# ScalarE's program as a loop over four packs, V loaded by one transfer per pack, and two kinds of transfer moved to SyncE's queue, in a cached two-block attention kernel

## The chip, the cores and the metric

One core of one Trainium2 chip. The time is device microseconds of one execution. Three runs of the kernel before took 739.08, 739.24 and 739.37 us, median 739.24. The profiled execution took 739.09 us, of which the profile's span covers 737.3.

## The reference

Two blocks A and B of the same form, with inputs of their own, side by side in the last dimension of the output. B = 16 batches, Sq = 64 queries, D = 640, H = 32 heads, Sk = 512 keys, Dh = 128, all bf16.

```
q = (x @ wq).reshape(B, Sq, H, Dh).transpose(0, 2, 1, 3)
scores = einsum("bhqd,bhkd->bhqk", q, k_cache) * Dh**-0.5
p = softmax(scores)
o = einsum("bhqk,bhkd->bhqd", p, v_cache)
out = o.transpose(0, 2, 1, 3).reshape(B, Sq, H * Dh) @ wo
```

The K and V caches of both blocks are 268 MB of the 292 MB that the kernel reads.

## The kernel before

**Packs, groups, phases.** A pack is two batches times four heads; there are 128, and each brings 1 MB of K and 1 MB of V. Four packs (NJ = 4) make a group: the same two batches, sixteen heads, one accumulated output. Eight groups (all 16 batches) make a phase of 32 packs: half of the heads of one block. Phases 0 and 1 are block A, 2 and 3 block B. Each phase has weights of its own: wq (five transfers LDWQ, put in order by POOL's WP) and wo (four transfers LDWO of 640 KB, one for each pack position).

**Operations of pack n.** LDK and LDV bring K and V (before: two transfers of 512 KB each, with K in four for the first eight packs). On TensorE: QP (query projection, L626), S (scores, L650), TR (transposes of the probabilities, L709), PV (L732), OP (output projection, L752), and once per group XT (transposes of x, L605). On VectorE: KT (two blockwise transposes of K, L640), RC (two reciprocals of row sums, L682), TE (two copies of the transposed probabilities out of PSUM, L719), once per group OS (the output's sum, L762 and L765). On ScalarE: QE (L632), four EX (exponentials with row sums, L669), two OE (L740), ZO (zeroes a PSUM region, L744), and XE (x out of PSUM, L611) in the groups of the first phase of each block. On POOL: four NM (probabilities times reciprocal, L698), once per group XC (L615). ST stores a group's output in phases 1 and 3.

**The order.** `build_plan` gives each operation a place in time, in units of one pack, from the table `AT` (S of pack n at n, TR at n + 1.293 and so on). Sorted by it, the operations make one fixed program for each engine; the loads make SP's program, sorted by keys given at `loads.append`. Each engine runs its program in order. TensorE's round is S(m), TR(m-1), OP(m-2), [XT,] QP(m+1), PV(m-1). VectorE's is KT(m+1), TE(m-1,0), RC, TE(m-1,1), RC. SP's interleaves V(n), K(n+3) and the rarer loads.

**Waits.** From what each operation reads and writes the planner derives dependencies, turns them into semaphore waits, drops those that others imply, and lets one wait stand in for another where the latter's semaphore is kept for TensorE (`stand_in`). Some waits are put on an earlier operation of another engine: the wait for wo stood on OE(n,1) on ScalarE, the wait for x and for WP on EX.

**Loops.** TensorE's program is a hardware loop of 32 turns over four packs (`Fori`); at each turn it lowers its semaphores by what one turn adds, so that every turn waits for the same values. The programs of the other engines are written out in full for all 128 packs.

**Rings.** K has six buffers (NK), V four (NV). A V buffer is free again when PV of the pack four before it is done, so SP's LDV(n) waits for PV(n-4). EX writes its probabilities into `p_ring`, and NM multiplies them into the one buffer `pn_sb`, which TR reads.

**Queues.** SP issues K, V, x, wq from phase 1 on, and wo of phase 0. ScalarE issues the first loads of x and wq, wo of phases 1 to 3 (L565) and all output stores (L771). They are two hardware queues, q1 and q10 in the profile, in front of the same sixteen DMA engines.

**The end.** The last two packs (NARROW) use another layout, and the last one is normalised by VectorE instead of POOL. In the program of before, its third and fourth NM stand behind its transposes: they start at 732.00 us, TR at 728.48.

Of the kernel before, what the change touches and what calls it, by code (L numbers as in the profile page):

```python
# [17 lines left out]
PARTS = dict(d_v=2)  # L18


class Cfg:
# [5 lines left out]
    NQ = 2  # L27
    NP = 4
    NR = 2
# [5 lines left out]
    AT = dict(XT=-2.585, XE=-2.383, XC=-0.788, QP=-0.428, QE=-0.224, KT=(-0.672, -0.65), S=0,  # L35
              EX=(0.307, 0.252, 0.358, 0.4), RC=(0.45, 0.6), RCO=0.48, NM=(0.803, 0.854, 1.088, 1.187),
              NMZ=(0.615, 1.231, 1.718, 1.794), TR=1.293, TE=(1.432, 1.47), PV=1.701, OE=(1.888, 2.013), ZO=2.221,
              OP=2.387, OS=2.576, LDWO=2.6, ST=3.559, WP0=-1.75, WP1=-1.596)
# [20 lines left out]
LOADS = ("LDK", "LDV", "LDX", "LDWQ", "LDWO")  # L59


def build_plan(dims, cfg, general):
# [18 lines left out]
    def add_output(n):  # L81
        g, j = n // NJ, n % NJ
        final = n >= 0 and dims["FINAL"](g // NBP)
        for b in range(2):
            tv = n + AT["PV"]
            op = add("sp", "LDV", (n, b), tv - 0.3, [], [("v" if n >= 0 else "absent", n % cfg.NV, b)])
            loads.append((n - cfg.NV + AT["PV"] + 0.2 if n >= 0 else -99.0, 3, op))
        if n > -2:
            add("pe", "TR", n, n + AT["TR"], [("pn", i) for i in range(4)] + [("ident",)], [("B", 4), ("B", 5)])
# [17 lines left out]
    for g in range(N // NJ + 1):  # L107
        n0 = g * NJ
        txt = n0 + AT["XT"]
        add("pe", "XT", g, txt, [("xn", g % cfg.NXN), ("ident",)], [("SB", 0)])  # L110
        if g == N // NJ:
            break
        if dims["FIRST"](g // NBP):
            add("act", "XE", g, n0 + AT["XE"], [], [("SB", 0), ("xs", g % NBP)])
            if g:
                loads.append((txt - 3.7, 0, add("sp", "LDX", g, txt - 0.5, [], [("xn", g % cfg.NXN)])))
            else:
                add("act", "LDX", g, -21.0, [], [("xn", g % cfg.NXN)])
        add("pool", "XC", g, n0 + AT["XC"], [("xs", g % NBP)], [("xT", g % cfg.NX)])
    for ph in range(NPH):  # L120
# [5 lines left out]
        for j in range(NJ):  # L126
# [5 lines left out]
            if ph:  # L132
                add("act", "LDWO", w, n0 - NJ + AT["LDWO"], [], [("wo", j)])
# [7 lines left out]
    add("pool", "NM", -1, -1 + AT["NM"][3], [], [("pn", i) for i in range(4)])  # L141
    for n in range(-2, N):
# [15 lines left out]
        for i in range(4):  # L158
            h = 4 * n + i
            te = n + AT["EX"][i]  # L160
            if general:
                add("dve", "MX", h, te - 0.002, [], [("SB", i), ("negmax", h % 4)])
            add("act", "EX", h, te, [("negmax", h % 4)] if general else [],
                [("SB", i), ("p", h % cfg.NP), ("rs", h)])
            add("pool" if n < N - 1 else "dve", "NM", h, n + (AT["NM"] if n < N - 1 else AT["NMZ"])[i], [("p", h % cfg.NP), ("recip", n % cfg.NR, i // 2)], [("pn", i)])
        for a in range(2):
            add("dve", "RC", (n, a), n + (AT["RCO"] if n % NJ == 1 and not a else AT["RC"][a]), [("rs", 4 * n + i) for i in (2 * a, 2 * a + 1)],
                [("recip", n % cfg.NR, a)])
    if not general:
        add("dve", "FL1", 0, N - 1 + AT["TE"][1] + 0.002, [("rs", h) for h in range(4 * N)], [("good",)])  # L170
# [25 lines left out]
    pe = progs["pe"]  # L196
    lo = next(i for i, o in enumerate(pe) if o.kind == "QP" and o.idx == 0)
    hi = next(i for i, o in enumerate(pe) if o.kind == "QP" and o.idx == cfg.PERIOD)
    size = hi - lo
    last_qp = max(o.idx for o in pe[lo:hi] if o.kind == "QP")  # L200
    reps = 1 + (N - 1 - last_qp) // cfg.PERIOD
    step = dict(XT=cfg.PERIOD // NJ, QP=cfg.PERIOD, S=cfg.PERIOD, TR=cfg.PERIOD, PV=cfg.PERIOD, OP=cfg.PERIOD)
    for k in range(reps):
        for i in range(size):
            o, o0 = pe[lo + k * size + i], pe[lo + i]
            assert o.kind == o0.kind and o.idx == o0.idx + k * step[o.kind], (k, i, o.kind, o.idx, o0.kind, o0.idx)
    loop = dict(lo=lo, size=size, reps=reps)
    inside = {id(o) for o in pe[lo:lo + size * reps]}

    for op in ops:  # L210
        if op.kind == "OP":
            at[("OE", (op.idx, 1))].deps += [d for d in op.deps if d.kind in ("LDWO", "WZ")]
            op.deps = [d for d in op.deps if d.kind not in ("LDWO", "WZ")]
        if op.kind == "XT" and op.idx > 0:
            at[("EX", 4 * (NJ * op.idx - NJ + 1))].deps += [d for d in op.deps if d.kind == "LDX"]
            op.deps = [d for d in op.deps if d.kind != "LDX"]
        if op.kind == "QP" and op.idx > 0:
            at[("EX", 4 * op.idx - 4)].deps += [d for d in op.deps if d.kind == "WP"]
# [4 lines left out]
    def for_pe(d):  # L223
        if d.kind == "EX":
            return d.idx % 4 == 1 or d.idx % 4 == 0 and d.idx // 4 % NJ == 1
        if d.kind == "OE":
            return d.idx[1] == 0
        if d.kind == "NM":
# [5 lines left out]
    def stand_in(d, op):  # L234
        if op.eng == "pe":
# [10 lines left out]
            return d  # L246
        if not for_pe(d):
# [23 lines left out]
    def sem_key(op):  # L271
        if op.kind in ("LDX", "LDWQ") and op.eng == "act":
            return ("d_first",) + op.writes[0]
        if op.kind == "LDV":
            return ("d_v", op.writes[0][1])
# [19 lines left out]
    per = periodic_waits(progs, loop)  # L295
    verify_waits(progs, base)
    loop["per"] = per
    loop["take"] = place_takes(progs["pe"][lo:lo + size], per)
    return progs, counts, loop


def place_takes(turn, per):


    spots = [i for i, o in enumerate(turn) if o.kind == "OP"] + [len(turn) - 1]
# [96 lines left out]
def periodic_waits(progs, loop):  # L402

    pe = progs["pe"]
# [41 lines left out]
def mha_kernel(nc, blocks, out, cfg=None):  # L446
# [24 lines left out]
    NK, NV, NKT, NX, NXN, NQ, NP, NR = (cfg.NK, cfg.NV, cfg.NKT, cfg.NX, cfg.NXN, cfg.NQ, cfg.NP, cfg.NR)  # L471

    with contextlib.ExitStack() as es:
# [11 lines left out]
        xT_ring = sb("xT_ring", [128, NX, KT, 128], BF16)  # L485
        xs_sb = sb("xs_sb", [128, NBP, KT * 128], BF16)
        xn_ring = sb("xn_ring", [128, NXN, D], BF16)
        qs_ring = sb("qs_ring", [128, NQ, 4, 2, 64], BF16)
        p_ring = sb("p_ring", [128, NP, 512], BF16)
        pn_sb = sb("pn_sb", [128, 16, 128], BF16)  # L490
        pT_sb = sb("pT_sb", [128, 2, 16, 64], BF16)
        oT_sb = sb("oT_sb", [128, 4, 128], BF16)
        zeros = sb("zeros", [128, 256], BF16)
        out_sb = sb("out_sb", [128, D], BF16)
        acc = sb("acc", [128, NBP, D], F32)
        rowsum = sb("rowsum", [128, NH], F32)
        negmax = sb("negmax", [128, 4], F32)
        recip = sb("recip", [128, NR, 4], F32)
# [7 lines left out]
        for p, (_progs, counts, _loop) in enumerate(plans):  # L506
# [71 lines left out]
        def em_LDV(e, op):  # L578
# [3 lines left out]
            blk, bp, j, h = pack_info(n)  # L582
            src = blocks[blk][2][2 * bp + b, h:h + 4]
# [26 lines left out]
        def em_XE(e, op):  # L610
            ins = e.activation(xs_sb[:, op.idx % NBP, :], x_ps[:, 0:KT * 128], ACTF.Copy)  # L611
            return ins, ins

        def em_XC(e, op):
            ins = e.tensor_copy(xT_ring[:, op.idx % NX].rearrange("p k q -> p (k q)"), xs_sb[:, op.idx % NBP, :])  # L615
# [44 lines left out]

        def exp_views(h):
            src, dst = ps[:, h % 4, :], p_ring[:, h % NP, :]
            u = 2 if wide(h // 4) else 4
            return (src.rearrange("q (u t p) -> q t p u", u=u, p=16), dst.rearrange("q (t p u) -> q t p u", p=16, u=u))

        def em_EX(e, op):
            h = op.idx
            src, dst = exp_views(h)
            ins = e.activation(dst, src, ACTF.Exp, scale=1.0, accum_out=rowsum[:, h:h + 1])  # L669
            return ins, ins  # L670

        def em_EXG(e, op):
# [3 lines left out]
            ins = e.activation(dst, src, ACTF.Exp, bias=negmax[:, r:r + 1], scale=1.0, accum_out=rowsum[:, h:h + 1])  # L676
            return ins, ins

        def em_RC(e, op):
            n, a = op.idx  # L680
            lo, hi = 2 * a, 2 * a + 2
            ins = e.reciprocal(recip[:, n % NR, lo:hi], rowsum[:, 4 * n + lo:4 * n + hi])  # L682
            return ins, ins

        def em_NM(e, op):
            h = op.idx
            i = h % 4
            if h < 0:
                ins = e.memset(pn_sb[:, :, :].rearrange("p t c -> p (t c)"), 0.0)
                return ins, ins  # L690
            if wide(h // 4):
                dst = pn_sb[:, :, 32 * i:32 * i + 32]
                src = p_ring[:, h % NP, :].rearrange("q (t k) -> q t k", t=16)
            else:
                a, s = i // 2, i % 2
                dst = pn_sb[:, 8 * a:8 * a + 8, 64 * s:64 * s + 64]
                src = p_ring[:, h % NP, :].rearrange("q (t k) -> q t k", t=8)
            ins = e.tensor_scalar(dst, src, recip[:, h // 4 % NR, i:i + 1], 1.0, ALU.mult, ALU.mult)  # L698
# [5 lines left out]
        def em_TR(e, op):  # L704
            first = last = None
            for c in range(16):
                for b in range(2):
                    rows = slice(64 * b, 64 * b + 64)
                    last = e.transpose(pt_bank(b)[:, 64 * c:64 * c + 64], pn_sb[rows, c, :], ident[rows, rows],  # L709
# [33 lines left out]
        def em_ZO(e, op):  # L743
            ins = e.activation(z_ps, zeros[:, :].rearrange("p (s c) -> p s c", s=2), ACTF.Copy)  # L744
# [31 lines left out]
        def em_FL1(e, op):  # L776
            first = e.tensor_reduce(extreme[:, 0:1], rowsum[:, :], AX.X, ALU.max)
            first.then_inc(s_ch, 1)
            e.tensor_reduce(extreme[:, 1:2], rowsum[:, :], AX.X, ALU.min).then_inc(s_ch, 1)
            e.wait_ge(s_ch, 2)  # L780
            e.tensor_scalar(extreme[:, 2:3], extreme[:, 0:1], SUM_MAX, None, ALU.is_le).then_inc(s_ch, 1)
            e.tensor_scalar(extreme[:, 3:4], extreme[:, 1:2], SUM_MIN, None, ALU.is_ge).then_inc(s_ch, 1)
# [37 lines left out]
        def run_program(e, eng, p):  # L820
            progs, counts, loop = plans[p]
            prog = progs[eng]
            if eng != "pe":
                for i, op in enumerate(prog):
                    if p == 0 and i == max(0, len(prog) - 300):
                        ahead[eng] = e.mark_branch_hint_location()
                    emit(e, op, p, {})
                return
            lo, size, reps, per = loop["lo"], loop["size"], loop["reps"], loop["per"]
            for key in sorted(counts):  # L830
                if key[0].startswith("q_"):
                    e.sem_inc(sems[p][key], cfg.BASE)
            for op in prog[:lo]:
                emit(e, op, p, {})
# [105 lines left out]
```

## Time and profile before

| | before |
|---|---|
| median of three runs | 739.24 us |
| profiled execution / its span | 739.09 / 737.3 us |
| busy: PE, DVE, ACT, POOL | 678.4, 521.8, 529.6, 404.0 us |
| DMA | 295.12 MB, mean 400 GB/s |
| V loads | 256 issues of 512 KB, 14.8 us (A) and 16.5 us (B) from issue to landing |
| wo loads by ScalarE's queue | 12 of 640 KB, 17.7 us (A) and 16.9 us (B) |
| output stores | 16 of 160 KB, 6.7 us |

A matmul group's busy time is modelled, so "PE busy 92%" does not say that TensorE is the bound. The DMA row counts how busy the sixteen DMA engines were on average: at 9 in every slice they had work all the time. "q14 instruction" and "q8 instruction" are the fetches of the engines' programs, which run on the same DMA engines. Semaphores tell when a transfer has landed: it counts sixteen increments, so a reader of the tile waits for the last of them.

### The profile page before, as it was taken

The page shows a single profiled execution, that of the slowest core. Times are in us where ns is not written, and L with a number is a line of the kernel's source. Part 1 is how long each engine was busy: PE and PEld are TensorE (multiplying, and loading weights), DVE is VectorE, ACT ScalarE, POOL GpSimd, SP SyncE. Part 2 cuts the span into 40 slices and gives each one's busy share as a digit, 9 for nine tenths or more (in the row PEclk, how much of TensorE's full clock was granted, in tenths as well). Part 3 has the DMA queues.
Part 4 walks back from the last instruction along what each step waited for, and adds up shares of the span by engine and source line. Part 5 has one row for each costly group of instructions (what it writes and reads, how often), then busy time and mean ns, then how long its engine had stood idle before and what let it go on. Part 6 is the DMA issues. An engine that isn't in the chain of part 4 may idle for free.

```text
span 737.3 us, 61335 instructions
## 1 busy us (share of the span) xinstructions
PE 678.4 (92%) x28502; PEld 531.3 (72%) x28502; DVE 521.8 (71%) x818; ACT 529.6 (72%) x1559; POOL 404.0 (55%) x580
## 2 busy tenths in 40 slices
PE   3669999999998999999988989999999799999997
PEld 2457787877776777777766767777777577878785
DVE  7437877877767767767765677768686577787775
ACT  2448888888776777767766777768777577777775
POOL 3635555556964455554684644555577455555451
PEclk9999999999999999999999999999999999999999
DMA  8999999999999999999999999999999999999991
GB/s 323 393 405 414 414 414 414 413 415 414 410 402 412 417 416 415 416 417 415 414 403 407 415 414 414 414 414 413 415 416 402 409 415 416 416 416 415 417 387 38
DMA packets 75995, 295.12 MB, mean 400 GB/s; under 512 B 9520, under 2 KB 24368, under 8 KB 59568
## 3 DMA queue, kind: packets, MB, share of 16 engines
q1 hardware_dynamic: 64544, 281.41, 94.4%
q10 hardware_dynamic: 11408, 13.27, 5.1%
q14 instruction: 33, 0.27, 0.1%
q8 instruction: 10, 0.16, 0.1%
HBM read 292.03 MB, written 2.62 MB: 400 GB/s over the span
## 4 chain that ended last, share of the span: by engine, by line
PE 47%; DMA 25%; SPq 12%; DVE 5%; POOL 4%; issue 3%; ACT 2%; ACTq 0%; POOLq 0%; DVEq 0%
DMA kn_ring<-in_B_k_cache_dram 15%; PE ps L732 13%; PE ps L752 11%; PE ps L626 10%; PE ps L650 8%; DMA kn_ring<-in_A_k_cache_dram 8%; SPq L586 6%; PE ps L709 5%; SPq L575 5%; DVE kt_ring L640 3%; DMA ws_sb<-in_A_wq_dram 2%; POOL pn_sb L698 2%; POOL wqp_sb L598 2%; DVE pT_sb L719 2%; ACT p_ring L669 1%
## 5 line engine op out<-in xcount | busy, mean ns | idle before, releaser
L698 POOL TENSOR_SCALAR pn_sb<-p_ring,recip 128x512 bf16<-128x512 bf16 x508 | 341.8, 692 | 302.7 <-DVE recip L682 302.6
L640 DVE STREAM_TRANSPOSE kt_ring<-kn_ring 128x1024 f32<-128x1024 f32 x256 | 302.8, 1222 | 123.5 <-DMA kn_ring<-in_B_k_cache_dram 85.3
L669 ACT ACTIVATE p_ring<-ps 128x512 bf16<-128x512 f32 x512 | 298.0, 596 | 9.5 <-PE ps L650 5.4
L719 DVE COPY pT_sb<-ps 128x1024 bf16<-128x1024 bf16 x258 | 169.6, 669 | 52.3 <-PE ps L709 52.1
L732 PE MATMUL ps<-pT_sb,v_ring 32*128 32x64 bf16 x16512 | 163.3, 192 | 30.9 <-DVE pT_sb L719 15.5
L732 PEld LDWEIGHTS ps<-pT_sb,v_ring 32*128 32x128 bf16 x16512 | 148.5, 91 | 46.5 <-issue 26.2
L626 PE MATMUL ps<-xT_ring,wqp_sb 128*128 128x128 bf16 x2560 | 166.4, 221 | 7.2 <-POOL xT_ring L615 7.2
L740 ACT ACTIVATE oT_sb<-ps 128x256 bf16<-128x256 f32 x260 | 85.7, 381 | 120.2 <-PE ps L732 119.5
L752 PE MATMUL ps<-wo_sb,oT_sb 128*128 128x320 bf16 x1040 | 166.8, 304 | 1.7 <-ACT ps L744 1.6
L626 PEld LDWEIGHTS ps<-xT_ring,wqp_sb 128*128 128x128 bf16 x2560 | 158.0, 114 | 13.6 <-issue 7.4
L650 PE MATMUL ps<-kt_ring,qs_ring 32*64 32x512 bf16 x4096 | 139.7, 383 | 3.0 <-issue 2.9
L632 ACT ACTIVATE qs_ring<-ps 128x512 bf16<-128x512 f32 x128 | 76.4, 597 | 62.7 <-PE ps L626 61.9
L752 PEld LDWEIGHTS ps<-wo_sb,oT_sb 128*128 128x128 bf16 x1040 | 92.1, 99 | 39.7 <-ACT ps L744 2.0
L709 PEld LDWEIGHTS ps<-ident,pn_sb 64*128 64x128 bf16 x4128 | 69.1, 96 | 63.9 <-ACT oT_sb L740 50.7
L669 ACT ACTIVATION_READ_ACCUMULATOR p_ring<-ps 128x1 f32 x512 | 105.8, 207 | 0.0
L709 PE MATMUL ps<-ident,pn_sb 64*128 64x64 bf16 x4128 | 84.2, 192 | 9.3 <-issue 3.9
L650 PEld LDWEIGHTS ps<-kt_ring,qs_ring 32*64 32x64 bf16 x4096 | 53.1, 103 | 31.9 <-issue 4.4
L682 DVE RECIPROCAL recip<-rowsum 128x2 f32<-128x2 f32 x256 | 40.5, 158 | 33.0 <-ACT p_ring L669 25.9
L744 ACT ACTIVATE ps<-zeros 128x256 f32<-128x256 bf16 x130 | 50.4, 388 | 4.1
L598 POOL COPY wqp_sb<-ws_sb 128x1280 bf16<-128x1280 bf16 x32 | 39.2, 1256 | 16.3 <-DMA ws_sb<-in_A_wq_dram 16.3
L615 POOL COPY xT_ring<-xs_sb 128x640 bf16<-128x640 bf16 x32 | 22.9, 716 | 0.3 <-PE ps L626 0.3
L605 PE MATMUL ps<-ident,xn_ring 128*128 128x128 bf16 x165 | 14.9, 222 | 3.8 <-DMA xn_ring<-in_A_x_dram 3.3
(26 smaller groups left out, 65.7 us busy)
## 6 DMA issues: line engine op xcount, KB each, us to landing
v_ring<-in_A_v_cache_dram SPq DMA_DIRECT2D x128, 512.0 KB, 14.8
kn_ring<-in_B_k_cache_dram SPq DMA_DIRECT2D x128, 512.0 KB, 16.8
v_ring<-in_B_v_cache_dram SPq DMA_DIRECT2D x128, 512.0 KB, 16.5
kn_ring<-in_A_k_cache_dram SPq DMA_DIRECT2D x112, 512.0 KB, 15.5
kn_ring<-in_A_k_cache_dram SPq DMA_DIRECT2D x32, 256.0 KB, 10.3
ws_sb<-in_B_wq_dram SPq DMA_DIRECT2D x10, 512.0 KB, 17.9
wo_sb<-in_B_wo_dram ACTq DMA_DIRECT2D x8, 640.0 KB, 16.9
ws_sb<-in_A_wq_dram ACTq DMA_DIRECT2D x4, 640.0 KB, 18.0
```

The lines of the kernel that those rows point to most:

```text
L598: last = e.tensor_copy(dst[:, :, :, jj], src[:, :, :, jj].rearrange("p k i (r two) -> p k i r two", two=2))
L626: last = e.matmul(ps[:, 1, f * 128:(f + 1) * 128], w[:, kt, f, :], xT_ring[:, xs, kt, :], start=(kt == 0), stop=(kt == KT - 1))
L632: ins = e.activation(qs_ring[:, op.idx % NQ].rearrange("p f b q -> p (f b q)"), ps[:, 1, :], ACTF.Copy, scale=scale)
L640: ins = e.transpose(dst.rearrange("p c b (h l) -> p c h b l", h=8, l=2), src)
L650: last = e.matmul(ps[64 * b:64 * b + 64, i, :], qs_ring[rows, n % NQ, f, b, :], kt_ring[rows, n % NKT, :, f // 2, b, :, f % 2], start=(f = ...
L669: ins = e.activation(dst, src, ACTF.Exp, scale=1.0, accum_out=rowsum[:, h:h + 1])
L698: ins = e.tensor_scalar(dst, src, recip[:, h // 4 % NR, i:i + 1], 1.0, ALU.mult, ALU.mult)
L709: last = e.transpose(pt_bank(b)[:, 64 * c:64 * c + 64], pn_sb[rows, c, :], ident[rows, rows], tile_position=(64 * b, 0))
L719: ins = e.tensor_copy(pT_sb[:, b].rearrange("p t q -> p (t q)"), pt_bank(b))
L732: last = e.matmul(ps[:, 4 + i, 64 * b:64 * b + 64], v_ring[rows, n % NV, b, c, :], pT_sb[rows, b, c, :], start=(t == 0 and i < 2), stop=(t ...
L740: ins = e.activation(oT_sb[:, 2 * a:2 * a + 2, :], o_ps[:, 2 * a:2 * a + 2, :], ACTF.Copy)
L752: last = e.matmul(out_ps[:, s, :], oT_sb[:, i, :], wo_sb[:, 4 * j + i, s * NH0:(s + 1) * NH0], start=(j == 0 and i == 0), stop=(j == NJ - ...
```

## The change

1. ScalarE's program becomes a loop of 26 turns over four packs (packs 0 to 103); the last 24 packs are written out (`AFTER = 24`). To make turns alike, XE now runs in every group, into a buffer `xe_sb` of its own, and POOL's new XS copies it to `xs_sb` in the first phase of a block.
2. What ScalarE issued inside these packs goes to SP: LDWO of phases 1 to 3 and ST. The wait for wo moves from OE(n,1) to TE(n,1) on VectorE, that for x from EX to POOL's NM, the one on WP goes.
3. V of packs 8 to 125 is one transfer of 1 MB, both batches together. SP's LDV(n) waits for TR(n-3) in the place of PV(n-4).
4. EX writes straight into `pn_ring` (two buffers), in pieces of 32 columns; NM multiplies in place.
5. The last pack's four NM stand ahead of its transposes. The final range test reads the reciprocals instead of the row sums; `zeros` is one column, read as a broadcast.

```diff
-    NQ = 2
-    NP = 4
-    NR = 2
+    NQ = 1
+    NPN = 2
+    NRS = 4
+    AFTER = 24
-              NMZ=(0.615, 1.231, 1.718, 1.794), TR=1.293, ...
-              OP=2.387, OS=2.576, LDWO=2.6, ST=3.559, ...
+              NMZ=(0.48, 0.49, 0.61, 0.62), TR=1.293, ...
+              OP=2.387, OS=2.576, LDWO=2.6, ST=2.8, ...
...
-        for b in range(2):
+        apart = 0 <= n < cfg.KSPLIT or n >= N - cfg.NARROW
+        for b in range(0 if apart else 1, 2):
...
-                add("act", "ST", g, n + AT["ST"], [("out_sb",)], [("out_dram", g)])
+                loads.append((n + AT["ST"], 5, add("sp", "ST", g, n + AT["ST"], [("out_sb",)], [("out_dram", g)])))
...
-        if dims["FIRST"](g // NBP):
-            add("act", "XE", g, n0 + AT["XE"], [], [("SB", 0), ("xs", g % NBP)])
+        first = dims["FIRST"](g // NBP)
+        add("act", "XE", g, n0 + AT["XE"], [], [("SB", 0), ("xe",)])
+        if first:
+            add("pool", "XS", g, n0 + AT["XS"], [("xe",)], [("xs", g % NBP)])
...
-                add("act", "LDWO", w, n0 - NJ + AT["LDWO"], [], [("wo", j)])
+                loads.append((n0 - NJ + AT["LDWO"], 4, add("sp", "LDWO", w, n0 + AT["OP"] - 0.8 * NJ, [], [("wo", j)])))
...
+    loops = {"pe": find_loop(progs["pe"], cfg.PERIOD, NJ, N, 0)}
+    if not general:
+        loops["act"] = find_loop(progs["act"], cfg.PERIOD, NJ, N, cfg.AFTER)
...
+        if op.kind == "PV":
+            at[("TE", (op.idx, 0))].deps += [d for d in op.deps if d.kind == "LDV" and not d.idx[1]]
+            op.deps = [d for d in op.deps if d.kind != "LDV" or d.idx[1]]
         if op.kind == "OP":
-            at[("OE", (op.idx, 1))].deps += [d for d in op.deps if d.kind in ("LDWO", "WZ")]
+            at[("TE", (op.idx, 1))].deps += [d for d in op.deps if d.kind in ("LDWO", "WZ")]
...
-            at[("EX", 4 * (NJ * op.idx - NJ + 1))].deps += [d for d in op.deps if d.kind == "LDX"]
+            at[("NM", 4 * (NJ * op.idx - NJ) + 3)].deps += [d for d in op.deps if d.kind == "LDX"]
...
+        if d.kind == "PV" and op.eng == "sp":
+            return at[("TR", d.idx + 1)]
+        if d.kind == "XT" and op.eng == "sp":
+            return at[("XE", d.idx)]
+        if d.kind == "OS" and op.eng == "sp" and for_pe(d):
+            return at[("RC", (d.idx * NJ + NJ + 1, 1))]
...
+            if wide(n) and n >= cfg.KSPLIT:
+                src = blocks[blk][2][2 * bp:2 * bp + 2, h:h + 4].rearrange("b h (p t) d -> (h p) b (t d)", t=16)
+                ins = e.dma_start(v_ring[:, n % NV].rearrange("p b t d -> p b (t d)"), src)
+                return ins, ins
...
+        def em_XS(e, op):
+            ins = e.tensor_copy(xs_sb[:, op.idx % NBP, :], xe_sb[:, :])
+            return ins, ins
...
-            ins = e.tensor_scalar(dst, src, recip[:, h // 4 % NR, i:i + 1], 1.0, ALU.mult, ALU.mult)
+            ins = e.tensor_scalar(pn_view(h), pn_view(h), recip[:, h:h + 1], 1.0, ALU.mult, ALU.mult)
...
+            if eng in loops:
+                lo, size, reps, per = (loops[eng][k] for k in ("lo", "size", "reps", "per"))
+                for op in prog[:lo]:
+                    emit(e, op, p, {})
+                with nc.Fori(0, reps, engines=[e.engine], head_slot={e.engine: 0}):
+                    for i, op in enumerate(prog[lo:lo + size]):
+                        emit(e, op, p, taken)
+                        ...
```

More of the change, by code (lines that the diff above doesn't have):

```diff
@@ L59, with find_loop, moved @@
 LOADS = ("LDK", "LDV", "LDX", "LDWQ", "LDWO")
+def find_loop(prog, period, nj, total, spare):
+    lo = next(i for i, o in enumerate(prog) if o.kind == "QP" and o.idx == 0 or o.kind == "QE" and o.idx == 0)
+    kind = prog[lo].kind
+    hi = next(i for i, o in enumerate(prog) if o.kind == kind and o.idx == period)
+    size = hi - lo
+    last = max(o.idx for o in prog[lo:hi] if o.kind == kind)
+    reps = 1 + (total - spare - 1 - last) // period
+    step = dict(XT=period // nj, XE=period // nj, EX=4 * period)
+    def moved(o, k):
+        if isinstance(o.idx, tuple):
+            return (o.idx[0] + k * period,) + o.idx[1:]
+        return o.idx + k * step.get(o.kind, period)
+    for k in range(reps):
+        for i in range(size):
+            o, o0 = prog[lo + k * size + i], prog[lo + i]
+            assert o.kind == o0.kind and o.idx == moved(o0, k), (k, i, o.kind, o.idx, o0.kind, o0.idx)
+    return dict(lo=lo, size=size, reps=reps)
 def build_plan(dims, cfg, general):
@@ L294, in build_plan, with place_takes @@
     order_waits(progs, need, base)
-    per = periodic_waits(progs, loop)
+    for eng, loop in loops.items():
+        loop["per"] = periodic_waits(progs, progs[eng], loop)
     verify_waits(progs, base)
[L297 to L305, printed above, removed]
+    for eng, loop in loops.items():
+        waiters = {e for e in ENGINES for o in progs[e] for s, _ in o.waits if s in loop["per"]}
+        assert waiters == {eng}, (eng, waiters)
+        body = progs[eng][loop["lo"]:loop["lo"] + loop["size"]]
+        assert all(v > 0 for o in body for _, v in o.waits)
+        loop["take"] = place_takes(body, loop["per"], "OP" if eng == "pe" else "ZO")
+    return progs, counts, loops
+def place_takes(turn, per, kind):
+    spots = [i for i, o in enumerate(turn) if o.kind == kind] + [len(turn) - 1]
     load = {i: 0 for i in spots}
@@ L399, in order_waits, with periodic_waits @@
     run_order(progs, visit)
-def periodic_waits(progs, loop):
-    pe = progs["pe"]
+def periodic_waits(progs, pe, loop):
     lo, size, reps = loop["lo"], loop["size"], loop["reps"]
@@ L505, in mha_kernel @@
         sems = []
-        for p, (_progs, counts, _loop) in enumerate(plans):
+        for p, (_progs, counts, _loops) in enumerate(plans):
             sems.append({key: es.enter_context(nc.semaphore("_".join([f"p{p}"] + [str(k) for k in key])))
@@ L820, in run_program @@
         def run_program(e, eng, p):
-            progs, counts, loop = plans[p]
+            progs, counts, loops = plans[p]
             prog = progs[eng]
[L823 to L826, printed above, removed]
-                    emit(e, op, p, {})
-                return
-            lo, size, reps, per = loop["lo"], loop["size"], loop["reps"], loop["per"]
@@ L830, in run_program @@
[L830 to L834, printed above, removed]
-            with nc.Fori(0, reps, engines=[e.engine], head_slot={e.engine: 0}):
-                taken = {}
-                for i, op in enumerate(prog[lo:lo + size]):
-                    emit(e, op, p, taken)
-                    for s, v in sorted(per.items(), key=str):
-                        if loop["take"][s] == i:
-                            e.sem_inc(sems[p][s], -v * units(s))
-                            taken[s] = v
```

135 lines of the change are left out of this document (71 added, 64 removed).

## The prediction

> **What bounds the kernel now.** I read the page's transfer rows first, then the waits, then windows, then the timeline around the last weight load.
>
> ```profile
> DMA  8999999999999999999999999999999999999991
> GB/s 323 393 405 414 414 414 414 413 415 414 410 402 412 417 416 415 416 417 415 414 403 407 415 414 414 414 414 413 415 416 402 409 415 416 416 416 415 417 387 38
> ...
> q14 instruction: 33, 0.27, 0.1%
> q8 instruction: 10, 0.16, 0.1%
> ```
>
> The sixteen DMA engines are busy in every slice between start and tail, at 402 to 417 GB/s. Instruction fetches are only 0.2% of the traffic; they come back below.
>
> ```profile
> DVE kt_ring L640 <- DMA kn_ring<-in_B_k_cache_dram: 85.3, 61, 3.6
> ...
> DVE kt_ring L640 <- DMA kn_ring<-in_A_k_cache_dram: 37.1, 29, 2.9
> ```
>
> VectorE waits 122 us for K, at nearly every pack from the 36th on.
>
> ```profile
> 240.00:365.00 125.00, 119.88 (x5078) 94.25 (x5077) 90.01 (x143) 92.79 (x276) 65.71 (x98) 1.00 1.02 416
> ...
> 545.00:600.00 55.00, 48.51 (x2110) 37.85 (x2098) 36.90 (x58) 37.08 (x111) 37.10 (x50) 1.00 1.03 409
> 600.00:715.00 115.00, 113.54 (x4901) 89.58 (x4901) 87.46 (x138) 89.77 (x268) 62.51 (x93) 1.00 1.02 415
> ...
> 718.00:719.00 1.00, 1.00 (x89) 0.78 (x84) 1.00 (x1) 0.38 (x2) 1.00 (x2) 1.00 0.44 168
> ...
> 722.00:724.00 2.00, 2.00 (x160) 1.69 (x165) 0.17 (x1) 1.04 (x4) 1.91 (x3) 1.00 0.09 33
> ```
>
> Columns: stretch, its length, then PE, PEld, DVE, ACT, POOL busy, clock, DMA share, GB/s. DMA share is 1.02 to 1.03 throughout. TensorE idles 6.5 us while the last phase's weights load (545 to 600) and only 1.5 us from 600 to 715. The last two rows show the stream running out: the share drops to 0.44 at 718, yet at 722 to 724 it is still 0.09, which is one engine or two of sixteen. Some engines run late, and a K tile counts as landed only when the last has delivered.
>
> The trace holds sixteen semaphore increments per transfer. Sorted within a K tile, the three latest stand behind the median (us):
>
> ```
> K tile near  third  second  slowest
>  257.8 us    0.65   0.74    1.16
>  318.3       0.98   1.18    2.44
>  427.2       1.40   1.97    3.23
>  481.5       1.43   2.65    3.90
>  530.4       2.37   3.29    4.54
>  588.1       2.34   3.96    5.21
>  711.4       3.28   5.25    6.51
> ```
>
> The slowest steps up by some 0.65 us at 259, 309, 363, 418, 473, 528, 634 and 682; the second steps with it from 363 on. At the instruction packets of those times ScalarE stands at its 581st, 701st, 833rd, 958th, 1090th, 1223rd, 1477th and 1599th instruction: 120 to 133 apart between neighbours (one more, at 579, is its 1345th). So ScalarE's unrolled program is fetched every 128 instructions, and each fetch holds up the same late engines.
>
> ```profile
> 575.49 2.37 DVE L640 STREAM_TRANSPOSE kt_ring<-kn_ring 128x1024 f32<-128x1024 f32 x2 [2.94 <-DMA kn_ring<-in_B_k_cache_dram]
> ...
> 578.43 0.67 DVE L719 COPY pT_sb<-ps 128x1024 bf16<-128x1024 bf16 x1
> ...
> 579.24 1.21 PE L732 MATMUL ps<-pT_sb,v_ring 32*128 32x64 bf16 x128 [1.46 <-DVE pT_sb L719]
> ...
> 580.38 1.07 PE L650 MATMUL ps<-kt_ring,qs_ring 32*64 32x512 bf16 x32
> ```
>
> This is the path where transfers bind: K lands, KT 2.37, the two TE copies of an older pack behind it on VectorE (the second is shown), PV 1.21, then S.
>
> **The change part by part.** The sum is made against the profiled execution: 739.09 us, 1.79 of it outside the 737.3 span, 0.15 below the median of 739.24.
>
> ScalarE's loop: 26 turns cover packs 0 to 103, so its fetches from about 55 to 575 us go; two or three stay for the last 24 packs. Without them the two late engines no longer lead the lateness; the third does. At 588 us that is 5.21 - 2.34 = 2.87 us of earlier landing, at 711 us 6.51 - 3.28 = 3.23. If another engine replaces them at once it is 0; if all engines fell to the median it would be 5.2. I take 2.8, the third engine being in the same rows.
>
> V by one transfer: 118 packs lose one of two issues, thus 16 four-byte completion packets each. In the trace these take 9.5 ns: 93 packs before 588 us x 9.5 = 0.9 us per engine, 1.1 by the end. [...]
>
> V's release: SP now waits for TR(n-3) instead of PV(n-4), which is S and TR later: PV ends 708.04, TR 709.62, 1.6 us. Behind it on SP stand K and the rest. V's landing took at least 7.2 us after issue, so the queues still hold over 5 us: nothing. Were they empty it would cost 1.6 us a pack.
>
> Weights wo by SP instead of ScalarE's own queue, and the wait for them moved from OE(n,1) to TE(n,1) on VectorE, ahead of RC and the next KT. In SP's order wo(96) to wo(99) stand behind K(99) to K(102). Near 588 us in-order service has moved as many bytes as before: wo(99) lands at 588.24, where K(102) landed, instead of 584.65. TE(99,1) started at 585.67, so it waits 2.6. Then 0.67 + 0.1 + 1.21 puts S(101) at 590.2 (was 587.75) and S(102), a TensorE round of 5.03 later, at 595.2 (was 593.88): +1.35. In the two earlier phases the same wait is swallowed, TensorE idling 5.1 us at 240 to 365 and 7.9 at 405 to 545. Bounds: 0 (wo as early as before) to +6.4 (one more K and V, 2 x 2.52, ahead of it).
>
> After S(102) TensorE runs at its own 5.03 (5.46 with XT). K then lands earlier than compute wants it, so its remaining idle time goes: 1.46 us in 594 to 700, of which I take 1.3.
>
> Output stores by SP: ST(g) stands behind K(n+7), which lands 0.6 before S(n+6); the next OS comes 3.3 after that S. It is released by RC, earlier than the next V's TR. No cost. LDX waits 1.1 us longer to issue, and NM waits for it in POOL; x lands about 0.4 behind K(n0-2), when that NM starts, and TR has 0.58 us in hand: 0 to 0.5 a group, taken as 0.
>
> XE in every group: 16 x 0.72 on ScalarE, into the 0.64 to 0.70 it idles before QE; QE ends 0.5 before S. XS: 16 x 0.72 on POOL, idle 2 to 3 us a pack; before QP(0) it is +0.7, lost again by 240. Turns of the loop: TensorE's 32 turns show no gap (XT 0.44 explains 5.46 against 5.03), and ScalarE idles 0.37 before QE, where its turn lies. EX in strides and NM in place: 597 and 692 ns; QE's plain write takes 597 too, and POOL's strided WP copy takes 0.98 ns an element against XC's plain 1.12, so 0. Up to 0.145 us per instruction is covered by the 0.58 before TR, and beyond that it costs four times the excess per pack. A gain there is equally hidden.
>
> Last pack: its four NM fit between TE (ends 726.75), RC (727.32) and 727.9; TR started at 728.48 behind OE: 0.
>
> Sum: -2.8 - 0.9 + 1.35 - 1.3 = -3.65, so 735.4 profiled and 735.6 for the median.
>
> **The rivals.**
> B, wo does not bind: in-order service lands it in time, as the ACT queue did (576.6 against TE(98,1) at 578.43). -3.65 - 1.35 = -5.0: 734.2. For: K lands earlier once wo no longer cuts in. Against: the order on SP. 0.10.
>
> C, another engine takes the slowest place at once: only completions count, -0.9 + 1.35 - 1.3 = -0.85: 738.4. Against: the third engine's 2.34. 0.10.
>
> D, slower: a V transfer now alternates between two batches 4 MiB apart, and its packets lengthen. 118 x 16 = 1888 packets of 162.8 ns per engine. 1.9 ns more each ends the gain, 2.7 ns makes it slower by over 0.2%; at 171 ns, what one packet in twenty takes now, +15.5: 751.1. Against: K's packets make the same 4 MiB step, and 8 KB take 315 ns, 26.0 GB/s, more than V's 25.2. [...] 0.08.
>
> E, slower: ScalarE fetches its body again each turn, 26 fetches instead of ten: 16 x 0.65 = 10.4 us more on the late engine and on K's landing: 739.24 + 10.4 - 0.9 (completions) = 748.7. Against: TensorE's queue 8 has no packet from 53.5 to 727.9 us. 0.06.
>
> F, slower: wo one more K and V late, 5.05 more at S(102): 740.6, and more if VectorE's wait also delays KT. 0.06.
>
> **How the numbers follow.** The forecast has 0.60. About 0.2% (1.5 us) is what a measurement tells from no change: forecast and B are faster, 0.70; C same, 0.10; D, E, F slower, 0.20. Range 733.2 (B with another 1 us of lateness gone) to 741.0 (F), leaving out D, E and the tails.
>
> **What would show it.** Right: fewer than 25 packets in queue 14; DMA share falling to 0 earlier after 718; 118 fewer V issues of 1 MB with V packets still near 163 ns; the lateness of the slowest engine near 3 us at 700; VectorE waiting for wo at TE near 580; S(102) near 591.6. Wrong: lateness still 5 to 6 us, longer V packets, fetches at every turn, DMA share below 1 in mid-run, or NM above 0.84 us.

## The result and the profile after

The new kernel takes 736.88 us (median of 8 runs, 736.34 to 738.63), the kernel before 739.31 us in the same comparison (8 runs, 738.87 to 739.77): a ratio of 0.9969, 95% interval [0.9960, 0.9978], 0.3% faster. The profiled execution took 736.34 us, its span 734.6 (before 739.09 and 737.3).

The transfer rows of the page after:

```profile
DMA  9999999999999999999999999999999999999991
GB/s 332 393 399 409 413 416 414 414 415 415 415 399 411 416 416 416 415 417 416 416 412 399 417 414 414 415 414 413 417 414 406 405 418 415 416 418 417 417 410 59
...
q8 instruction: 10, 0.16, 0.1%
q14 instruction: 24, 0.20, 0.1%
```

The stream is as full as it was, and 9 of the 33 fetch packets of queue 14 are gone: the loop does not fetch its body at every turn (rival E falls). The waits of VectorE for transfers (us in total, times, longest):

```profile
DVE kt_ring L686 <- DMA kn_ring<-in_B_k_cache_dram: 40.3, 43, 2.3
...
DVE kt_ring L686 <- DMA kn_ring<-in_A_k_cache_dram: 27.4, 23, 2.5
...
DVE pT_sb L768 <- DMA wo_sb<-in_B_wo_dram: 17.1, 8, 3.2
...
DVE pT_sb L768 <- DMA wo_sb<-in_A_wo_dram: 6.2, 4, 2.3
```

VectorE waits 68 us for K where it waited 122, and 23 us at a place where it waited for no transfer before: TE waits for wo at every one of the 12 loads that moved. The stretches (length, then PE, PEld, DVE, ACT, POOL busy, clock, DMA share, GB/s):

```profile
240.00:365.00 125.00, 121.06 (x5144) 95.34 (x5129) 91.37 (x145) 96.74 (x289) 67.80 (x100) 1.00 1.02 416
...
545.00:600.00 55.00, 46.93 (x2031) 37.02 (x2024) 36.92 (x57) 37.75 (x113) 35.09 (x46) 1.00 1.03 409
600.00:715.00 115.00, 115.00 (x4950) 91.19 (x4951) 92.86 (x142) 92.75 (x278) 64.78 (x96) 1.00 1.02 416
718.00:719.00 1.00, 1.00 (x16) 0.88 (x14) 0.88 (x3) 1.00 (x5) 0.55 (x1) 1.00 0.38 146
...
722.00:724.00 2.00, 1.62 (x38) 1.01 (x30) 1.46 (x4) 2.00 (x8) 0.00 (x0) 1.00 0.04 11
```

From 600 to 715 us TensorE is busy without a gap (113.54 of 115 before); from 545 to 600 it idles 8.1 us instead of 6.5, and that is where wo loads. The last two rows show the stream run out slightly earlier: the DMA share is 0.38 at 718 and 0.04 at 722, where it was 0.44 and 0.09. The timeline around the last load of wo (start, duration, engine, line, idle time before and what ended it):

```profile
582.89 0.69 DVE L768 COPY pT_sb<-ps 128x1024 bf16<-128x1024 bf16 x1 [0.64 <-PE ps L758]
...
586.02 0.69 DVE L768 COPY pT_sb<-ps 128x1024 bf16<-128x1024 bf16 x1 [2.22 <-DMA wo_sb<-in_B_wo_dram]
...
586.70 2.35 DVE L686 STREAM_TRANSPOSE kt_ring<-kn_ring 128x1024 f32<-128x1024 f32 x2
...
586.86 1.21 PE L781 MATMUL ps<-pT_sb,v_ring 32*128 32x64 bf16 x128 [1.71 <-DVE pT_sb L768]
...
588.00 1.07 PE L696 MATMUL ps<-kt_ring,qs_ring 32*64 32x512 bf16 x32
```

TE(99,1) now starts when wo(99) has landed, at 586.02, and KT stands behind it without a wait: K was there. S(101) follows TE(99,1) by 1.98 us, the 0.67 + 0.1 + 1.21 of the prediction. From the semaphore increments of the raw trace, sorted as in the prediction, and from the starts of S:

```
                     slowest engine behind the median, us     S(102)   S(127)  execution
                     near 427   near 588   near 711           us       us      us
before                3.23       5.21       6.51              593.88   723.50  739.09
after                 2.63       3.52       3.89              593.31   720.78  736.34
```

V's packets are as long as they were (4096 bytes: 163.0 ns, before 162.8; rival D falls), and 1888 completion packets are gone: 118 transfers by 16.

One execution is not the kernel. A second profiled execution of the new kernel took 737.76 us. Its slowest engine is 3.37 us late near 588 and 3.63 near 711, but S(102) is at 594.78 and S(127) at 722.21, 1.5 and 1.4 later than in the first. One round makes the difference: the granted clock of TensorE is 0.50 from 588.4 to 591.6 us, and S(102) follows S(101) by 6.86 us where it takes 5.31 in the first. Such a stretch of 3.4 us is worth 1.55 us here, more than half of the gain of the whole change. S(102) and S(127) below are of single executions; of the other traces only that of the looped padding has such a stretch in this round.

### The profile page after: what moved, and what is told of

It is laid out like the page before. It is cut to its first block, busy times and chain, and to the rows that moved or that the text cites. A ratio compares the mean times of both kernels' runs of the same rounds, so it can differ in the third digit from the quotient of the medians.

```text
span 734.6 us, 61314 instructions
## 1 busy us (share of the span) xinstructions
PE 673.0 (92%) x28502; PEld 529.7 (72%) x28502; DVE 526.3 (72%) x818; ACT 532.7 (73%) x1575; POOL 416.3 (57%) x596
## 4 chain that ended last, share of the span: by engine, by line
PE 57%; DMA 29%; SPq 6%; DVE 3%; issue 2%; POOL 2%; ACT 0%; ACTq 0%; DVEq 0%
PE ps L781 13%; PE ps L801 13%; PE ps L672 11%; PE ps L696 11%; DMA xn_ring<-in_B_x_dram 9%; PE ps L758 7%; DMA kn_ring<-in_A_k_cache_dram 7%; DMA wo_sb<-in_B_wo_dram 6%; SPq L612 4%; DMA kn_ring<-in_B_k_cache_dram 2%; DMA ws_sb<-in_A_wq_dram 2%; DMA wo_sb<-in_A_wo_dram 2%; DVE kt_ring L686 1%; SPq L622 1%; DVE pT_sb L768 1%
## 5 line engine op out<-in xcount | busy, mean ns | idle before, releaser
L746 POOL TENSOR_SCALAR pn_ring<-pn_ring,recip 128x512 bf16<-128x512 bf16 x508 | 342.1, 692 | 247.8 <-DVE recip L738 242.8
L725 ACT ACTIVATE pn_ring<-ps 128x512 bf16<-128x512 f32 x512 | 296.1, 592 | 4.3 <-PE ps L696 4.3
L768 DVE COPY pT_sb<-ps 128x1024 bf16<-128x1024 bf16 x258 | 171.7, 676 | 103.1 <-PE ps L758 79.5
L758 PEld LDWEIGHTS ps<-ident,pn_ring 64*128 64x128 bf16 x4128 | 68.9, 95 | 71.0 <-ACT oT_sb L789 48.4
L725 ACT ACTIVATION_READ_ACCUMULATOR pn_ring<-ps 128x1 f32 x512 | 105.7, 206 | 0.0
L758 PE MATMUL ps<-ident,pn_ring 64*128 64x64 bf16 x4128 | 83.9, 191 | 17.2 <-POOL pn_ring L746 8.0
L652 ACT ACTIVATE xe_sb<-ps 128x640 bf16<-128x640 bf16 x32 | 23.0, 718 | 1.5 <-PE ps L646 1.4
L661 POOL COPY xT_ring<-xe_sb 128x640 bf16<-128x640 bf16 x16 | 11.5, 716 | 20.6 <-PE ps L758 20.6
```

The costliest lines, as they stand in the source:

```text
L746: ins = e.tensor_scalar(pn_view(h), pn_view(h), recip[:, h:h + 1], 1.0, ALU.mult, ALU.mult)
L758: last = e.transpose(pt_bank(b)[:, 64 * c:64 * c + 64], pn[rows, c, :], ident[rows, rows], tile_position=(64 * b, 0))
L768: ins = e.tensor_copy(pT_sb[:, b].rearrange("p t q -> p (t q)"), pt_bank(b))
```

## The experiments

In the four sets of runs the kernel before took 739.37, 739.43, 739.29 and 739.69 us. "Ratio" is that to the kernel before. The new kernel itself, run again beside others, gave 736.78 us (5 runs, 736.25 to 737.90), ratio 0.9964 [0.9950, 0.9977].

> The changed kernel itself, for comparison inside this call: 736.9, slowest engine's lateness near 4 us at 700.

**What the loop is worth.** ScalarE's program written out again, all else new:

```diff
-        loops["act"] = find_loop(progs["act"], cfg.PERIOD, NJ, N, cfg.AFTER)
+        pass
```

> The changed kernel with ScalarE's program written out again; all else as changed. Fetch theory (ScalarE's fetches hold up the latest DMA engines): queue 14 goes from 24 packets back to about 33, the slowest engine's lateness near 700 us from 3.9 back to about 6 us, wo(99) and with it S(102) come 1.5 to 2.2 us later, and TensorE, the bound after that, keeps the loss: about 738.7 us, 1.8 more than with the loop. Queue theory (the gain is from wo and the stores standing behind K in one queue, not from the loop): 736.9, no difference.

738.66 us (11 runs, 737.22 to 740.69), ratio 0.9989 [0.9980, 0.9998]. Without the loop 1.8 of the 2.4 us are lost. In its trace:

```profile
q14 instruction: 32, 0.26, 0.1%
```

Eight fetches are back, and the slowest engine is 6.19 us late near 588 and 6.84 near 711. Two things stay as in the new kernel: VectorE waits 70 us for K (41.0 and 28.7) and not 122, and the 25 packs behind S(102) take 127.64 us. So these two are not the loop's doing. That a fetch, and not some other effect of the loop, costs the time is tested next: always-met waits are added to ScalarE's program, seven ahead of QE and seven ahead of OE(n,0), 14 a pack, once with the program written out and once with the loop. Apart from the loop's own branches both kernels execute the same instructions.

```diff
+        s_pad = es.enter_context(nc.semaphore("s_pad"))
...
+            if op.eng == "act" and op.kind in ("QE", "OE") and (op.kind == "QE" or op.idx[1] == 0):
+                for _ in range(7):
+                    e.wait_ge(s_pad, 1)
```

> ScalarE's program written out, with 14 waits a pack added that are always met (7 ahead of QE, 7 ahead of the first OE; 17 ns each, 0.24 us a pack in idle time of ScalarE). Only the length of the program changes, from some 14 to 28 instructions a pack, so ScalarE's fetches double to about 27. Fetch theory: queue 14 at 45 or more packets, the slowest engine's lateness near 700 us above 12 us, and K and wo late by as much: 743 to 748 us. If fetches do not matter and the loop gains by something else: as the written-out kernel, 738.7.

> The same 14 waits a pack inside ScalarE's loop: the same instructions executed, no more fetched until the last 24 packs. Fetch theory: 737 to 737.5, lateness near 4 us. If the added waits themselves cost, this loses as much against the changed kernel as the padded written-out one does against the unpadded.

The padded program written out: 743.39 us (5 runs, 742.69 to 744.24), ratio 1.0051 [1.0037, 1.0065]. Looped: 736.69 us (6 runs, 736.22 to 740.74), ratio 0.9962 [0.9948, 0.9975]. The padding costs 4.7 us when it has to be fetched and nothing when it does not. The lateness rose less than expected (8.50 us near 575, 8.93 near 711; above 12 was expected), and so did the packets of queue 14 (40, where 45 or more were expected); the time came out inside the expected 743 to 748. The instruction rows, written out and then looped:

```profile
q14 instruction: 40, 0.33, 0.1%
```

```profile
q14 instruction: 27, 0.21, 0.1%
```

The only trace of the looped one is of the longest of its six executions, 740.74 us; the other five took 736.22 to 736.76. In it the slowest engine is 5.72 us late near 588 and 6.07 near 711, where near 4 was expected, and the granted clock is 0.50 from 591.3 to 594.5 us, with 6.86 us from S(101) to S(102). So the time of this kernel is as expected, and its lateness in an execution of that time was not seen.

In the trace after, the remaining steps of the slowest engine, 0.9 to 1.0 us each, stand at 277.6, 389.8, 500.6 and 615.8 us, where VectorE is at its 309th, 439th, 564th and 693rd instruction. So the same padding was put into VectorE's program in the new kernel, ahead of the first KT and of TE(n,0):

```diff
+            if op.eng == "dve" and op.kind in ("KT", "TE") and op.idx[1] == 0:
+                for _ in range(7):
+                    e.wait_ge(s_pad, 1)
```

> The new kernel with 14 waits on an always-met semaphore added to VectorE's program per pack (7 ahead of the pack's first KT, 7 ahead of TE(n,0), both places where VectorE idles), 1792 instructions in all, written out, as many as ScalarE's written-out program got in the padded run. Theory (after the loop on ScalarE, VectorE's program is the one whose fetches hold up the slowest DMA engines, so any written-out program has this price): queue 14 goes from 24 packets to 32 to 38, the slowest engine's lateness at a K tile near 588 us from 3.5 to above 5.5 us, and the time goes up by 2 to 6.5 us, to 738.8 to 743.3 (ScalarE's unrolled program cost 4.7 us with the same padding). Rival (VectorE's fetches fall on engines with slack, the price was peculiar to ScalarE): 736.3 to 737.3, as the new kernel. A rise without a rise of the lateness would mean that the waits themselves hold VectorE.

743.19 us (5 runs, 742.89 to 744.15), ratio 1.0048 [1.0034, 1.0062]: 6.4 us more, as much as the padded ScalarE program lost to its looped twin (6.7). Its instruction row and its waits:

```profile
q14 instruction: 32, 0.26, 0.1%
```

```profile
DVE kt_ring L686 <- DMA kn_ring<-in_B_k_cache_dram: 54.4, 46, 2.7
...
DVE kt_ring L686 <- issue: 8.2, 30, 1.0
```

The second row is idle time ahead of KT in which VectorE waited for nothing that the profile shows. I take it for the padding itself, at 30 of 256 KT some 0.3 us each, 23 of them ahead of 242 us; a like row ahead of TE (18.8 us, 8 times) lies wholly ahead of 68 us. It cannot be told apart fully from the rest, as VectorE's program was not run padded in a loop, but lateness and delay go together:

```
                     slowest engine, us        S(102)   S(127)   execution
                     near 588   near 711       us       us       us
after                 3.52       3.89          593.31   720.78   736.34
ScalarE written out   6.19       6.84          596.75   724.39   739.95
 " and padded         6.39       8.93          599.21   728.04   743.65
VectorE padded        8.86      11.03          599.39   728.61   744.15
```

With VectorE padded the slowest engine is 5.3 us later near 588 and S(102) 6.1; near 711 it is 7.1 later and S(127) 7.8. The slowest engine steps up by about 1.0 us at fetches some 128 of VectorE's instructions apart. The theory that a program fetch holds up single DMA engines and that each K tile waits for the last of them stands, for either engine's program.

In the new kernel's trace the packets of queue 8 have 16 KB (10 packets, 0.16 MB) and those of queue 14, to which the steps belong, 8 KB (24 packets, 0.20 MB); the four at VectorE's steps come 125 to 130 of its instructions apart. With the DMA engines full, at 416 GB/s, these fetches are not hidden, and ScalarE's program is 1.8 us faster as a loop than written out, 6.7 us with the padding.

**V by one transfer.** Always two again, with ScalarE's loop:

```diff
-        apart = 0 <= n < cfg.KSPLIT or n >= N - cfg.NARROW
+        apart = n >= 0
...
-            if wide(n) and n >= cfg.KSPLIT:
+            if False:
```

> The changed kernel with V of every pack by two transfers of 512 KB. If completions cost what their packets take (9.5 ns x 118 a DMA engine): 0.9 us later at S(102), 737.8. If a completion is free, or a doubled number of V issues on SP does not matter: 736.9. If V's rows 4 MiB apart had cost anything, this would be faster and V packets shorter than 163 ns.

737.60 us (11 runs, 736.96 to 739.17), ratio 0.9983 [0.9974, 0.9992]: 0.7 us more, though the intervals of the two ratios overlap. The page's packet rows, this kernel's and then the new one's:

```profile
DMA packets 75988, 295.06 MB, mean 401 GB/s; under 512 B 9520, under 2 KB 24368, under 8 KB 59568
```

```profile
DMA packets 74098, 295.04 MB, mean 402 GB/s; under 512 B 7632, under 2 KB 22480, under 8 KB 57680
```

The difference is the 1888 completions; 118 per engine at 9.5 ns are 1.1 us, of which 0.7 is seen. The medians lean to a price per completion, the intervals do not settle it. To find whether the price per transfer holds, K of every pack was brought by four transfers instead of two, 3840 more completions (`if True:` in the place of `if i < 2 or n < cfg.KSPLIT:` and of `if n < cfg.KSPLIT:` in K's loads):

> The changed kernel with K of every pack by four transfers of 256 KB in the place of two of 512 KB (as its first eight packs): 240 more completions on each DMA engine, the same bytes in the same 8 KB packets. If a completion costs its packet's 9.5 ns: 1.8 us by S(102), 738.7. If completions are free: 736.9. More than 739.5 would say that an issue costs more than its completion (SP, or the start of a transfer).

740.03 us (11 runs, 739.08 to 742.16), ratio 1.0008 [0.9999, 1.0017]: 3.2 us more, where 240 completions an engine at 9.5 ns make 2.3. One stretch of it:

```profile
600.00:715.00 115.00, 114.93 (x4804) 90.21 (x4790) 87.80 (x138) 89.93 (x268) 62.70 (x94) 1.00 1.01 411
```

The profiled execution was the longest of its eleven, 742.16 us, with the clock at 1.00 in this stretch. The stream moves 411 GB/s instead of 416 and TensorE is nearly always busy, yet its rounds without XT take 5.15 to 5.34 us instead of 5.03: PV takes some 1.36 us instead of 1.22, in rounds where KT starts 0.2 us ahead of it. More than completions is at work there; what, stays open.

**V's release.** ScalarE written out, and SP's LDV(n) waiting for PV(n-4) again, to be read against the written-out kernel alone:

```diff
-        if d.kind == "PV" and op.eng == "sp":
-            return at[("TR", d.idx + 1)]
```

> ScalarE's program written out, and SP's V waits for PV(n-4) as before, not for TR(n-3). To be compared with the written-out kernel of this call. If V's release does not matter (the DMA queues hold over 5 us): no difference between the two, within 0.5 us. If the 1.6 us later release costs DMA work: this one is faster by 1 us or more.

738.07 us (11 runs, 737.48 to 739.42), ratio 0.9983 [0.9974, 0.9992], against 0.9989 [0.9980, 0.9998]: 0.6 us, just over the 0.5 that was expected at most, with intervals that overlap. The release costs little or nothing.

**The place of wo.** In the new kernel wo stands behind K(n+3) in SP's order. It was put ahead of that K (2.35), and ahead of V too (1.85):

```diff
-              OP=2.387, OS=2.576, LDWO=2.6, ST=2.8, ...
+              OP=2.387, OS=2.576, LDWO=2.35, ST=2.8, ...
```

> The changed kernel with wo's key 2.35 instead of 2.6, so that SP issues wo(n) ahead of K(n+3), not behind it. If TE's wait for wo is what starts the last stretch late (my +1.35 of the sum): the wait of 3.1 us a pack at 565 to 586 us shrinks by about 2.5, S(102) comes up to 2.5 earlier and the TensorE-bound rest follows: 734.6 to 735.5. If the pace of the DMA engines in that stage decides and the wait only shows it: 736.9, with the wait moved to K.

> The changed kernel with wo's key 1.85: SP issues wo(n) ahead of V(n) and K(n+3) both. The run with wo ahead of K alone cut TE's wait for wo from some 3 to 0.6 us at the later packs of the stage, and K was waited for again. If the wait for wo is what starts the last stretch late, nothing more is to be had: 736.2, the same as with wo ahead of K. If the order of the transfers is free as long as the DMA engines are full, also 736.2; if holding V and K back behind OP costs, 737 or more.

Ahead of K: 736.18 us (5 runs, 735.39 to 736.80), ratio 0.9955 [0.9941, 0.9969], the lowest of all kernels run, though its interval overlaps that of the new kernel. Ahead of both: 736.73 us (6 runs, 735.35 to 738.69), ratio 0.9963 [0.9951, 0.9975]. The waits of the first:

```profile
DVE kt_ring L686 <- DMA kn_ring<-in_B_k_cache_dram: 74.5, 62, 2.7
...
DVE kt_ring L686 <- DMA kn_ring<-in_A_k_cache_dram: 36.4, 27, 2.5
...
DVE pT_sb L768 <- DMA wo_sb<-in_B_wo_dram: 9.0, 7, 2.3
```

The wait for wo falls from 23 to 10 us and that for K rises from 68 to 111. S(102) comes 1.4 us earlier (591.9), but the 25 packs after it take 128.7 us instead of 127.5 because K is late again; S(127) gains 0.15. With wo ahead of both VectorE waits for wo no more and 122 us for K (83.5 and 38.4), as before the change. Whichever transfer stands first, the other one is waited for.

**How much is written out.** The loop to the last four packs, alone and with wo ahead of K:

```diff
-    AFTER = 24
+    AFTER = 4
```

> The changed kernel with the loop going on until 4 packs from the end (31 turns). Fetch theory: it saves ScalarE's two or three last fetches, but these come after 575 us, when TensorE is the bound and K is early: 736.6 to 736.9. If the end of the loop itself costs (its place moved from 580 us, where TensorE waits anyway, to the end, where it doesn't): up to 1 us slower, 737.8.

> wo ahead of K (2.35) and the loop until 4 packs from the end, together. With wo ahead of K compute follows K's landing again, so lateness counts to the end: the last two or three fetches saved are worth up to 0.7 us: 735.5. If not: 736.2.

739.49 us (11 runs, 738.31 to 741.18), ratio 1.0002 [0.9993, 1.0010]; and 738.83 us (11 runs, 738.46 to 740.32), ratio 0.9996 [0.9987, 1.0005]. The first misses the theory's 736.9 by 2.6 us, and also the 737.8 that was allowed for a cost of the loop's end; the second misses 736.2, the higher of its two numbers, by 2.6. S(127) is at 721.01 and 720.87, within 0.25 us of the new kernel, and the last instruction that counts as work is early too. From the timelines of the new kernel and of `AFTER = 4`:

```profile
732.28 0.14 DVE L841 CAST flag<-ps 1x1 int32<-1x1 f32 x1
```

```profile
732.50 0.14 DVE L841 CAST flag<-ps 1x1 int32<-1x1 f32 x1
```

So 0.2 us of the loss lies ahead of this line, and the rest behind it. The raw trace shows the branch with which every engine ends its program, and the drain after it:

```
                ScalarE: branch, drain      SyncE: last drain      span
after           732.97   733.44             734.39                 734.6
AFTER = 4       733.19   736.87             734.61                 737.2
```

ScalarE needs 3.7 us from its last branch to the next instruction instead of 0.5, and the span ends 0.3 us behind that drain. I infer that the instruction behind the branch was not at hand: queue 14 has packets at 628.44 and 679.87 us in the new kernel that `AFTER = 4` lacks. No packet between the branch and the drain can be told to be ScalarE's, so this is not shown. ScalarE's one BRANCH_PREFETCH_HINT stands at 599.83 us in the new kernel and at 702.09 with `AFTER = 4`, right behind the loop each time; that its place is the reason was not tried.

## Why the prediction was right, and where not

The forecast was 735.6 us, range 733.2 to 741.0, with faster at 0.7; 736.88 came. Its path was the right one: K, KT, TE, PV, S on the late side of the DMA engines, then TensorE's own pace. By its four terms, on the profiled executions (S(102) moved by -0.57 us, the 25 packs behind it by -2.15):

```
term                                predicted   measured
ScalarE's fetches gone                -2.8       -1.7    slowest engine near 588: 5.21 to 3.52
V's completions                       -0.9       -0.7    two transfers again, medians
wo behind K                           +1.35      +1.8    by difference: what is left of S(102)'s -0.57
TensorE's idle time after S(102)      -1.3       -2.15   127.47 us instead of 129.62
sum                                   -3.65      -2.75   span: -2.7
```

The third row is a difference, so the first three add up to S(102) by construction and prove nothing as a sum. In the second execution of the new kernel they would add up to +0.90, 1.55 of it in the round at half clock. What tests the terms singly are the runs above and the readings below.

**The first term was mis-sized.** The step that failed is "the third does", that with ScalarE's fetches gone the slowest place falls to the third engine's 2.34 us. In the trace of before no lasting step of the slowest engine stands at VectorE's fetches (283.2, 393.3, 508.8, 620.7 us); two of them raise the third, from 1.40 to 2.32 at 508.8 and from 2.35 to 3.27 at 620.7, so 0.9 of the 2.34 came from a fetch that stayed. In the trace after each of VectorE's fetches is a step of the slowest engine, at 500.6 and 615.8 also of the second, and the third is at 1.21 near 588. Rival C was thus half right: another program's fetches took the slowest place, as the padded VectorE shows, at 3.52 us and not at 5.21. Why they met engines with slack before and not after was not settled. Nor was the prediction's list of steps whole: the slowest engine of before also rises from 3.03 to 3.78 behind a fetch at 371.8, which is none of ScalarE's, and falls back to 2.47 by 418, so not all lateness stays. The marker "near 3 us at 700" came out at 3.9.

**The third term was right in kind.** TE(99,1) waited for wo near 580 us as forecast, at 586.02, where the prediction's 588.24 less the two measured gains gives 585.8. S(101) followed by the 1.98 us that it used. Then the prediction gave S(102) a round of 5.03 us, and this round has an XT and takes 5.31: 0.28 more, and with the 0.2 at TE that makes the 1.8. "S(102) near 591.6" was 593.31. With wo ahead of K the wait nearly goes and the time moves by 0.7 at most, so rival B's full 1.35 was not to be had: K takes the place.

**The fourth term was too small.** 1.46 us of idle time were seen and 1.3 taken. The rounds with XT got shorter as well, 5.31 instead of 5.46 us; the prediction took 5.46 for TensorE's own pace and explained it by XT's 0.44. But QP starts 0.28 behind XT in both traces, and the other 0.15 stood between QP and PV (1.36 us near 612, after 1.21). Six such rounds at 0.15 give the missing 0.9. The term does not come from the loop, as the kernel with ScalarE written out has it too (127.64 us). It comes with wo's place: with wo ahead of K more than half of it is lost again (128.73), and with wo behind K, apart from padding and K by four, the 25 packs take 127.4 to 127.7 us, TensorE's own pace (19 rounds of 5.03 and 6 of 5.31 make 127.4). The third and the fourth term are thus two sides of one trade.

**What was costed at nothing** stayed there by the trace. NM took 692 ns, EX 592 (596 before), XE and XS stood beside other work, and SP held the stores. V's release changed nothing that can be told apart. The loop (1.8) and V's transfers (0.7) make 2.5 us where the whole change brought 2.4, so the remaining parts, wo's place and the last pack's NM among them, sum to about nothing, as far as these medians tell. Rivals D, E and F fell by V's packets, queue 14 and S(102).

## What to carry to other kernels

Where all DMA engines are full, as at 416 GB/s here, count the program fetches: an engine's written-out program is traffic that made single DMA engines late by 0.65 to 1.0 us a fetch, and K's tiles waited for the latest of them (6.51 us behind the median near 711 before, 3.89 after), so a loop on an engine that is off the path can shorten the path (1.8 us here). Look at the lateness of single engines and not only at the mean share (1.02 before and after), and size the gain from below, since another program's fetches can take the place (3.52 us near 588 where 2.34 was forecast). Moving a rare transfer within the full stream passed its wait to another (wo ahead of K: 23 to 10 us for wo, 68 to 111 for K). Before reading half a microsecond from two traces, compare the granted clock of the stretch (3.4 us at 0.50 were worth 1.55 us).

## What the runs showed that was not expected

- A fetch packet of 8 KB takes 0.31 to 0.34 us in the stream of the new kernel, but each of VectorE's makes the slowest engine 0.9 to 1.0 us later; why it costs three times its own length was not settled.
- 1792 always-met waits cost 4.7 us (ScalarE) and 6.4 us (VectorE) written out, and nothing in ScalarE's loop (736.69 us).
- A loop that ends four packs before the program's end leaves ScalarE 3.7 us at its final branch instead of 0.5.
- A stretch of 3.4 us at half clock in the round of S(102) made the second profiled execution 1.4 us longer than the first.
- K by four transfers costs 3.2 us, more than its completions, with TensorE's rounds longer while it waits for no K.
